# First unit's operands in tiles that are free early, more spare buffers where the left operands change, and reloaded sums in six half tiles

## The chip, the cores and the metric

The kernel runs on one core of a Trainium2 chip. A core has a matrix engine, TensorE (PE in the profile; its weight loads are PEld), and VectorE (DVE), ScalarE (ACT) and GpSimd (POOL), which work beside it in queues of their own and wait for each other by semaphores. SyncE (SP) only issues transfers, and POOL issues some too; the profile calls these two queues SPq and POOLq. Each queue runs its instructions strictly in the order in which the program wrote them. The metric is the device time of one execution in microseconds (us), lower is better. The kernel before takes 2368.73 us (median of 3 runs, 2366.69 to 2369.68).

## The reference

A gate mixes an attention branch and an MLP branch, over one sequence x of 2048 tokens and 1024 features:

```python
x = A_x                                                    # [1, 2048, 1024]
g = sigmoid((x * gate_w).sum(-1, keepdims=True))
# A: linear attention, 32 heads of 32, learned feature map
qkv = (x @ wqkv) split into q, k, v                        # wqkv [1024, 3072]
pq, pk = q @ w_phi, k @ w_phi                              # per head
phi = concat(softmax(p), softmax(-p))                      # for q and for k
kv, z = sum_s phi_k^T v, sum_s phi_k
a = (phi_q kv) / (phi_q z + 1e-6) @ wo                     # wo [1024, 1024]
# B: GEGLU
b = (gelu(x @ w_gate) * (x @ w_up)) @ w_down               # 1024 -> 3584 -> 1024
out = g * a + (1 - g) * b
```

All is float32. The kernel keeps that precision by splitting each operand into a high and a low part (`high` copies to the rounded type on ACT, `low` subtracts on DVE) and making each product in three passes: high by high, high by low, low by high.

## The kernel before, in words

**Units.** In its first part (0 to 1679 us) the kernel multiplies x by all columns of the weights for q, k, v, gate and up. After the plain products of the first 28 us (L289) the work is cut into 79 units: a unit is a pair of 128-column weight blocks by one half of the sequence. Each unit uses a Strassen-like scheme with seven products in place of eight. Its right operands, made from the weights, are x, y and z, whole tiles of 128 by 2048 values, and v, a half tile. Its left operands, made from x, are called x10, s1, s2, x11, s3, s4 and x01, a high (h) and a low (l) tile each. A product (`product`, L751) is twelve matmuls with 512 columns: four blocks of the inner dimension by three passes. The seven products go into PSUM banks named a, b, c, c11 and p, and the results of one unit seed the next: ACT copies c11 from a (L798), b from a (L800), c from b (L783), and takes p out into a tile w (L769); the second product of a unit writes the bank p again, so it waits for that copy.

**Turns.** The left operands belong to one half of the sequence and one form. Units 1 to 7 (v) are half 0, units 8 to 15 (k) half 1, units 16 to 47 half 2 (the first pass over q, gate and up), units 48 to 79 half 3 (the second pass, with the same weights). At units 8, 16 and 48, which I call turns, all seven left operands are replaced while the products go on: `PLANS` says for each one at which slot (a seventh of a unit, about 2.8 us) its float32 source is loaded, and into which home, a tile that is free just then; `change_parts` and `low_part` then split it on ACT and DVE, four pieces each.

**Sums.** In the first pass the sums x, y, z, v of each weight pair are made on DVE (L136 to L144) and stored to DRAM; the second pass loads them again. The tiles of y and z come from `slot()` (three buffers, named tyz), those of x from `new_weight()` (two buffers, named wgu). `load_part` (L596) brings y and z in two halves.

**Between the products** PE runs fillers: folds of the key and query weights with the feature matrix (L303, L443, L861), the key features times v (L971), and the attention (L1175). In the second part, from L1431 on, the output products follow, with left operands from the attention and the MLP.

**Who sets the order.** A planner in Python (`run_slot`) writes the instructions of ACT, DVE and SP beside the products. Streams (generators) offer their next step with the first slot in which it may stand, the slot in which it is due, and its estimated time on DVE and ACT; clocks of the planner decide in which slot it is written. The list `extra` places the work of the first two units by hand. An instruction written early waits at the head of its queue, and everything behind it waits too.

Of the kernel before, what the change touches and what calls it, by code (L numbers as in the profile page):

```python
# [8 lines left out]
F32 = mybir.dt.float32  # L9
# [7 lines left out]
P = 128  # L17
# [16 lines left out]
def tile_gated_mix(ctx: ExitStack, tc: tile.TileContext, x, xT, wkT, wqT, wv, w_phi, wo,  # L34
# [151 lines left out]
    with tc.manual_schedule(engines={PE, DVE, ACT, SP}):  # L186
# [140 lines left out]
        def first_sums(part):  # L327
            o, make, t = (first_o, quarter_sums, y1) if part == "y" else (first_e, more_sums, slot())
            first[part] = t
            make(first_e, first_o, True)  # L330
            high(flat(t)[0], o)
            low(flat(t)[1], o, flat(t)[0])

        def split_sums(*ks, kcs=range(1, 4)):
            for k in ks:
                for kc in kcs:
                    for do in sum_parts(k, kc):
                        do()

        def first_x():  # L340
            high(flat(x1)[0], first_e)
            low(flat(x1)[1], first_e, flat(x1)[0])

        first_x()
        for i in range(2):
            fold_piece(i)
        first_sums("y")
        for i in range(2, 4):
            fold_piece(i)
        sum_steps(100, 1)  # L350
        split_sums(0, kcs=range(4))
# [19 lines left out]
        def run_slot(t, matmuls=12, vector=0.0, scalar=0.0):  # L371
# [49 lines left out]
        def key_folds(i, groups):  # L421
            yield 14 + 4 * i, NEVER, 0.0
# [4 lines left out]
            for kc in groups:  # L427
                pieces = [(1, kc), (1, kc + 4), (0, kc), (0, kc + 4)]
                for (h, c), t in zip(pieces, four):
                    nc.sync.dma_start(t, wkT[h, c] if kc else wk_fold[h][c])  # L430
                yield now[0] + 2, NEVER, 0.0
                for n, ((h, c), t) in enumerate(zip(pieces, four)):
                    if kc == 0:
                        break
# [29 lines left out]
        def gates(pa):  # L464
# [7 lines left out]
            at = {}  # L472
# [10 lines left out]
        def change_half(t, half):  # L483
# [12 lines left out]
            for i, at, home in PLANS[half]:  # L496
                yield t + at, t + at, 0.0
                while home in busy:
                    yield now[0] + 1, now[0] + 1, 0.0
# [7 lines left out]
                busy[home] = True  # L507
# [10 lines left out]
        def home_parts(half, home):  # L518
            if half == 1:
                return (parts_of(work) if home == "y" else  # L520
                        [shared["pa"][:, n, BLK * m:BLK * m + BLK] for n in range(2) for m in range(2)])
# [265 lines left out]
        def unit(n, half, kind, m, before, extra={}):  # L787
# [5 lines left out]
            for k in range(7):  # L793
# [10 lines left out]
                for do in more_work:  # L804
                    do()
# [667 lines left out]
```

## Time and profile before

| | us |
|---|---|
| median of 3 runs (range) | 2368.73 (2366.69 to 2369.68) |
| the profiled execution | 2370.22 |
| its span, first to last instruction | 2368.4 |
| PE busy in the span | 2325.5 |
| DVE, ACT, POOL busy | 1744.5, 1210.1, 388.7 |
| mean granted TensorE clock | 0.992 |
| transfers | 645.70 MB, mean 273 GB/s |

The profiled execution's own time lies 1.5 us above the median, and its span is 1.8 us shorter than that time. PE is the engine to read: where it is idle the span grows, and where the granted clock is half, 128 by 512 matmuls start about 427 ns apart, otherwise about 227 ns. A wait is put down to the instruction that released it.

### The profile page before, as it was taken

To read this page: it belongs to the slowest core of one execution; us is meant where nothing else is said; L and a number is where in the kernel's file an instruction comes from. 1 tells how busy PE (TensorE), PEld (TensorE's weight loads), DVE (VectorE), ACT (ScalarE), POOL (GpSimd) and SP (SyncE) were. 2 spreads that over 40 slices of the span, in tenths; PEclk is the share of its full clock that TensorE was granted. 3 is DMA by queue.
4 is the path that set the end of the run, shared out by engine and by line. 5 is a ranking of instruction groups with operands and counts; after the bars stand their busy time and mean duration, and the time that the engine had idled before them with its cause. 6 is when DMAs were issued, how large, how long until landed. Compare 5 with 4: busy or idle time off the path is not lost. (4 is left out here: it accounts for less than half of the span.)

```text
span 2368.4 us, 29632 instructions
## 1 busy us (share of the span) xinstructions
PE 2325.5 (98%) x10414; PEld 1925.8 (81%) x10414; DVE 1744.5 (74%) x2394; ACT 1210.1 (51%) x1702; POOL 388.7 (16%) x618
## 2 busy tenths in 40 slices
PE   8999998999999999989999999999999999999999
PEld 6788887888888888877888888888888888888887
DVE  7667657888888887755888889875574868867873
ACT  5446346565656565543877777876433322323221
POOL 1443321222222222212111111111000000000000
PEclk9999999999999999999999999999999999999999
DMA  5689988888889999887888788877784767977874
GB/s 192 237 307 340 319 275 314 309 295 305 299 306 300 303 306 302 284 300 260 257 262 259 253 257 261 263 249 234 276 296 164 275 224 247 338 267 276 293 261 138
DMA packets 263749, 645.70 MB, mean 273 GB/s; under 512 B 32032, under 2 KB 68400, under 8 KB 255664
## 3 DMA queue, kind: packets, MB, share of 16 engines
q1 hardware_dynamic: 204592, 428.41, 54.4%
q0 software_dynamic: 58736, 215.27, 25.7%
q8 instruction: 82, 1.34, 0.2%
q14 instruction: 67, 0.55, 0.1%
q10 hardware_dynamic: 272, 0.13, 0.0%
HBM read 428.74 MB, written 215.23 MB: 272 GB/s over the span
## 5 line engine op out<-in xcount | busy, mean ns | idle before, releaser
L1431 PE MATMUL po<-tw,wgu 128*128 128x512 f32 x1344 | 309.8, 389 | 0.0
L56 ACT ACTIVATE wgu<-stage 128x1024 fp32r<-128x1024 f32 (+2 forms) x166 | 172.6, 1040 | 256.6 <-DVE stage L1321 160.9
L1431 PEld LDWEIGHTS po<-tw,wgu 128*128 128x128 f32 x1344 | 252.3, 188 | 52.4
L59 DVE TENSOR_TENSOR wgu<-stage,wgu 128x1024 fp32r<-128x1024 f32 (+2 forms) x135 | 161.5, 1196 | 87.1 <-ACT wgu L56 86.2
L751 PE MATMUL a<-s2h,tyz 128*128 128x512 f32 x632 | 212.5, 397 | 12.9 <-ACT tyz L56 5.0
L751 PE MATMUL p<-s1h,tyz 128*128 128x512 f32 x624 | 208.6, 396 | 14.0 <-DVE tyz L59 7.8
L751 PE MATMUL c<-x11h,wgu 128*128 128x512 f32 x632 | 209.7, 393 | 6.0 <-ACT x11h L56 4.3
L751 PE MATMUL c<-x01h,tyz 128*128 128x512 f32 x632 | 208.2, 390 | 0.2 <-ACT c L783 0.2
L751 PE MATMUL a<-s4h,v 128*128 128x512 f32 x632 | 208.4, 391 | 0.0
L751 PE MATMUL a<-x10h,wgu 128*128 128x512 f32 x632 | 207.9, 390 | 0.3 <-DVE wgu L59 0.3
L751 PE MATMUL b<-s3h,tyz 128*128 128x512 f32 x624 | 205.7, 390 | 0.0
L1431 PE MATMUL po<-tw,wl 128*128 128x512 f32 x672 | 156.9, 389 | 0.0
L1431 PE MATMUL po<-tyz,wgu 128*128 128x512 f32 x672 | 155.2, 389 | 0.0
L751 PEld LDWEIGHTS a<-s2h,tyz 128*128 128x128 f32 x632 | 120.4, 191 | 41.1 <-ACT tyz L56 5.4
L751 PEld LDWEIGHTS p<-s1h,tyz 128*128 128x128 f32 x624 | 118.8, 191 | 40.9 <-DVE tyz L59 9.2
L1431 PEld LDWEIGHTS po<-tw,wl 128*128 128x128 f32 x672 | 126.1, 188 | 26.2
L1431 PEld LDWEIGHTS po<-tyz,wgu 128*128 128x128 f32 x672 | 126.1, 188 | 26.2
L751 PEld LDWEIGHTS c<-x11h,wgu 128*128 128x128 f32 x632 | 119.8, 190 | 31.4 <-ACT x11h L56 4.7
L751 PEld LDWEIGHTS c<-x01h,tyz 128*128 128x128 f32 x632 | 118.8, 188 | 25.4 <-ACT c L783 0.7
L751 PEld LDWEIGHTS a<-s4h,v 128*128 128x128 f32 x632 | 119.1, 189 | 24.8
L751 PEld LDWEIGHTS a<-x10h,wgu 128*128 128x128 f32 x632 | 118.6, 188 | 25.2 <-DVE wgu L59 0.8
L751 PEld LDWEIGHTS b<-s3h,tyz 128*128 128x128 f32 x624 | 117.6, 188 | 24.1
(438 smaller groups left out, 4863.4 us busy)
## 6 DMA issues: line engine op xcount, KB each, us to landing
stage<-lm SPq DMA_DIRECT2D x98, 512.0 KB, 4.4
sr<-in_w_down SPq DMA_DIRECT2D x84, 512.0 KB, 5.0
sl<-lm SPq DMA_DIRECT2D x70, 512.0 KB, 4.7
lm<-h POOLq DMA_DIRECT2D x112, 256.0 KB, 5.7
stage<-in_w_gate SPq DMA_DIRECT2D x42, 512.0 KB, 6.7
stage<-in_w_up SPq DMA_DIRECT2D x42, 512.0 KB, 5.7
vs<-vt SPq DMA_DIRECT2D x32, 512.0 KB, 3.4
zs<-w POOLq DMA_DIRECT2D x32, 512.0 KB, 7.5
```

Source lines behind the costliest of these rows:

```text
L56: nc.scalar.activation(dst, src, AF.Copy)
L59: nc.vector.tensor_tensor(dst, src, dst_h.bitcast(F32), OP.subtract)
L751: nc.tensor.matmul(dst, w[:, h, 4 * part + kc, :], xq[e][:, kc, :], start=first and kc == 0 and i == 0, stop=kc == 3 and i == 2, skip_grou ...
L1431: nc.tensor.matmul(ps[c], lefts[s][:, a, m, c * P:(c + 1) * P], made[k][:, e, m], start=d == 0 and m == 0 and n == 0, stop=d == n_duo - 1 ...
```

## The change

**The first unit.** The x operand's high and low parts go into a tile of the pool `fa` (name s4h) in place of a weight tile, and z into a weight tile in place of a tyz tile. A fifth piece of the key weights, (1, 1), is folded early, in the tile o2. The four fold pieces no longer stand in one block behind the plain products: two pieces follow the first product, two the second, one the fourth. In the first unit the product p = s1 y stands in the third slot and not in the sixth. `extra` lists the work with costs, and the planner's clocks start at other values.

**The turns.** `PLANS` is written anew for the three turns, with other slots and homes: w is the tile `work`, y in halves 1 and 2 the shared early tile, x in half 2 three gated tiles and a tile wq. `change_parts` waits one slot more between load and split. The gates are spread over more slots; the first key features come no earlier than two slots after the turn to half 2 and not while w or y is in use. Key folds of the second kind start at slot 24 and not 18; query folds are 8/3 slots apart and not 5/3. Loads of values (`late_values`) become steps of their own.

**The second pass.** `load_part` and its callers go; a stream `reloads` loads y and z for all units from 49 on into six half tiles, each two slots after its last use. `product` then takes a half tile where there is one.

**Attention** starts later: its sums are loaded six slots after they are finished.

```diff
+        first_o = stage((0, 1024, block("v", 3)))
         room = stage().rearrange("p (a b) -> p a b", a=2)
-        first_o = stage((0, 1024, block("v", 3)))
         homes = [t[:, n] for t in (room, xa.tile([P, 2, BLK], F32, tag="v", name="fold", bufs=1)) for n in range(2)]
-        early_folds = [(h, c) for h in (1, 0) for c in (0, 4)]
+        homes.append(fa.tile([P, BLK], F32, tag="o2", name="fold", bufs=1))
+        early_folds = [(h, c) for h in (1, 0) for c in (0, 4)] + [(1, 1)]
...
-        x1 = new_weight()
         y1 = xa.tile([P, 2, KC, P], F32R, tag="pts", name="first", bufs=1)
         for i in (1, 2, 4, 5):
-            x_ops[0, i] = [x_part(i, part) for part in range(2)]
+            x_ops[0, i] = [x_part(i, part) if i != 5 else None for part in range(2)]
+        x1 = fa.tile([P, 2, KC, P], F32R, name="s4h", bufs=1)
...
+        def first_high(part, src):
+            if part == "z":
+                first[part] = new_weight()
+            high(flat(first[part])[0], src)
+
+        def first_low(part, src):
+            low(flat(first[part])[1], src, flat(first[part])[0])
+
+        def sums_high(k, *kcs):
+            if x_ops[0, (1, 2, 4, 5)[k]][0] is None:
+                x_ops[0, 5] = [x_part(5, part) for part in range(2)]
+            for kc in kcs:
+                sum_parts(k, kc)[0]()
+
+        def sums_low(k, *kcs):
+            for kc in kcs:
+                sum_parts(k, kc)[1]()
+
+        first_high("x", first_e)
+        first_low("x", first_e)
+        sums_high(0, 0, 1, 2)
+        quarter_sums(first_e, first_o, True)
+        first_high("y", first_o)
+        sums_low(0, 0, 1, 2)
         sum_steps(100, 1)
-        split_sums(0, kcs=range(4))
+        sums_high(0, 3)
+        first_low("y", first_o)
+        sums_low(0, 3)
...
-                    d *= 0.95
+                    d *= 0.97
...
-            yield 14 + 4 * i, NEVER, 0.0
+            yield 14 + 10 * i, NEVER, 0.0
...
-                yield max(now[0], at[c] + 3), NEVER, 1.3
+                yield max(now[0], at[c] + 3, begin + 9 * c // 8), NEVER, 1.3
...
-                while home in busy:
+                while home in busy or half == 2 and (gating[0] if home in ("w", "y") else folding[0]):
...
-        held_homes = []
-        SPARE = ((0, -7, "x"), (1, -6, "y"), (2, -4, "x"), (3, -3, 2), (4, -1, "y"))
-        PLANS = {1: (*SPARE, (6, 0, "x"), (5, 3, "y")), 3: (*SPARE, (6, 0, "g"), (5, 3, "z")),
-                 2: ((0, -11, "x"), (2, -5, 1), (1, -5, "x"), (3, -1, "x"), (4, 0, 3), (5, 3, 6), (6, 4, "x"))}
+        held_homes, gating = [], [True]
+        PLANS = {1: ((0, -9, "x"), (1, -8, "w"), (2, -5, "x"), (3, -4, "w"), (4, -1, "x"), (6, 1, "w"), (5, 3, "x")),
+                 2: ((0, -9, "w"), (1, -8, "y"), (2, -5, "w"), (3, -5, "x"), (4, -4, "y"), (6, 0, "w"), (5, 3, "x")),
+                 3: ((0, -7, "x"), (1, -5, "y"), (2, -4, "x"), (3, -3, "z"), (4, -1, 3), (5, 0, "g"), (6, 3, "z"))}
...
+                if j == 3 and raw[3] is raw[0]:
+                    yield now[0] + 3, need - 2, 0.0
...
-                else:
-                    yield max(now[0], t - 4), t - 4, 0.0
-                    y = mine["y"] = slot()
-                    load_part("y", y, 0)
-                    yield max(now[0], t - 2), t - 2, 0.0
-                    load_part("y", y, 1)
...
-            else:
-                yield t, t, 0.0
-                z = mine["z"] = slot()
-                load_part("z", z, 0)
-                yield t + 1, t + 1, 0.0
-                load_part("z", z, 1)
...
+        def reloads(n):
+
+            uses = sorted((7 * m + at, m, i, part) for m in range(n, len(units))
+                          for at, i, part in ((1, "y", 0), (3, "z", 0), (6, "y", 1), (9, "z", 1)))
+            rooms, t = [], 7 * n
+            last = len(uses) - 1
+            for k, (at, m, i, part) in enumerate(uses):
+                before = k - 6 if k < last - 1 else k - 4
+                if k < 6:
+                    if k % 2 == 0:
+                        yield t + (-4, 1, 4)[k // 2], NEVER, 0.0
+                        while k == 0 and "y" in busy:
+                            yield now[0] + 1, NEVER, 0.0
+                        whole = slot()
+                        rooms += [whole[:, :, 4 * h:4 * h + 4] for h in range(2)]
+                    room = rooms[k]
+                else:
+                    yield uses[before][0] + 2, NEVER, 0.0
+                    room = rooms[k % 6] = rooms[before % 6]
+                nc.sync.dma_start(room.rearrange("p a b c -> p a (b c)").bitcast(F32),
+                                  sums[units[m][1:]][i].rearrange("p (a b) -> p a b", a=2)[:, :, BLK * part:BLK * part + BLK])
+                right_ops[m][i, part] = room
...
+                elif k == 2:
+                    product(n, p, "y", 0, 1, half, True)
                 elif k == 3:
                     product(n, a, "z", 0, 2, half)
                 elif k == 4 and before:
                     product(n - 1, unit_banks[n - 1][0], "v", 0, 5, before[0])
-                elif k == 5:
-                    product(n, *((c11, "x", 1, 3, half) if before else (p, "y", 0, 1, half, True)))
+                elif k == 5 and before:
+                    product(n, c11, "x", 1, 3, half)
...
-                yield max(now[0], 62 + 5 * n // 3), NEVER, 0.0
+                yield max(now[0], 60 + 8 * n // 3), NEVER, 0.0
...
-                if fjobs and now[0] >= fjobs[0][0] and not folding[0]:
+                if fjobs and now[0] >= max(fjobs[0][0], 7 * TURNS[1] + 2) and not folding[0] and not {"w", "y"} & set(busy):
...
+            def late_values(after):
+                loaded[0] = False
+                yield now[0] + 1, now[0] + 1, 0.0
+                load_values(*after)
+                loaded[0] = True
...
+            sums_at[0] = now[0] + 6
...
-        tensor[0] = 35.0
-        clock[:] = 47.0, 42.0
-
-        outs, puts = ([lambda n=n, at=at, do=do: do(n, *at) for n, at in enumerate(((1, 0), (0, 1), (0, 0), (1, 1)))]
-                      for do in (plain_out, plain_store))
+        start(reloads(TURNS[-1] + 1))
+        tensor[0] = 22.0
+        clock[:] = 25.0, 23.6
+
+        outs, puts = ([(lambda n=n, at=at, do=do: do(n, *at), *cost) for n, at in enumerate(((1, 0), (0, 1), (0, 0), (1, 1)))]
+                      for do, *cost in ((plain_out, 0.0, 0.6), (plain_store, 0.84, 0.8)))
+        folds = [(lambda i=i: fold_piece(i), 0.0, 0.6, 0.95) for i in range(len(homes))]
         extra = {
             1: {0: [outs[0]],
-                1: [outs[1], lambda: sum_steps(100, 3), lambda: split_sums(1, 2, 3, kcs=(0,)), lambda: first_sums("z"), lambda: split_sums(1)],
-                2: [outs[2], outs[3]],
-                4: [lambda: split_sums(2)],
-                5: [lambda: sum_steps(1), lambda: split_sums(3, kcs=(1,))]},
-            2: {0: puts[:2], 1: [lambda: sum_steps(100), lambda: split_sums(3, kcs=(2, 3))], 2: puts[2:]}}
+                1: [*folds[:2], (lambda: more_sums(first_e, first_o, True), 1.4), (lambda: first_high("z", first_e), 0.0, 1.05),
+                    (lambda: sum_steps(2, 3), 1.4), (lambda: first_low("z", first_e), 1.2), (lambda: sum_steps(100, 3), 2.8),
+                    outs[1], (lambda: sums_high(1, *range(4)), 0.0, 2.4), (lambda: sums_low(1, *range(4)), 2.6)],
+                2: [*folds[2:4], (lambda: sums_high(2, *range(4)), 0.0, 2.4), (lambda: sum_steps(1), 0.7),
+                    (lambda: sums_high(3, 0), 0.0, 0.6), (lambda: sums_low(2, *range(4)), 2.6), (lambda: sums_low(3, 0), 0.7)],
+                4: [*folds[4:], outs[2], outs[3]]},
+            2: {1: [(lambda: sum_steps(1), 0.7), (lambda: sums_high(3, 1), 0.0, 0.6), (lambda: sums_low(3, 1), 0.7)],
+                2: [(lambda: sum_steps(100), 1.4), (lambda: sums_high(3, 2, 3), 0.0, 1.2), (lambda: sums_low(3, 2, 3), 1.4)],
+                3: puts[:1], 5: puts[1:2]},
+            3: {1: puts[2:3], 2: puts[3:]}}
```

What follows are rows of the three queues at the places of which the prediction speaks, in the order in which each queue runs them. The first is ACT's queue behind the plain products, before; `tyz<-stage` is the high part of z, `first<-stage` that of y, `s1h` to `s4h` are left operands, and `stage<-misc`, `fold<-misc` take the folds out.

```order
L56 ACTIVATE wgu<-stage 128x1024
L56 ACTIVATE stage<-misc 128x512 x2
L56 ACTIVATE first<-stage 128x1024
L56 ACTIVATE fold<-misc 128x512 x2
L56 ACTIVATE s1h<-raw 128x512 x4
L56 ACTIVATE w_545<-c_85 128x512
L798 ACTIVATE c_85<-a 128x512
L56 ACTIVATE w_545<-b 128x512
L56 ACTIVATE s2h<-raw 128x512
L56 ACTIVATE s3h<-raw 128x512
L56 ACTIVATE s4h<-raw 128x512
L56 ACTIVATE tyz<-stage 128x1024
```

And now:

```order
L56 ACTIVATE s4h<-stage 128x1024
L56 ACTIVATE s1h<-raw 128x512 x3
L56 ACTIVATE first<-stage 128x1024
L56 ACTIVATE s1h<-raw 128x512
L56 ACTIVATE w_547<-c_85 128x512
L815 ACTIVATE c_85<-a 128x512
L56 ACTIVATE stage<-misc 128x512 x2
L56 ACTIVATE wgu<-stage 128x1024
L56 ACTIVATE w_547<-b 128x512
L56 ACTIVATE s2h<-raw 128x512 x3
```

The folds' copies moved behind the copy of c11, and z's high part (now in wgu) stands ahead of the pieces of s2, s3 and s4.

The second place is ACT's queue at the turn to half 3, before; `x01h<-w` are the pieces of the left operand x01, `w_544<-p` frees the bank p.

```order
L56 ACTIVATE x01h<-w_544 128x512
L800 ACTIVATE b<-a 128x512
L56 ACTIVATE x01h<-w_544 128x512 x3
L56 ACTIVATE s4h<-stage 128x512 x4
L723 ACTIVATE h<-c_85 128x512
L769 ACTIVATE w_544<-p 128x512
```

And now:

```order
L817 ACTIVATE b<-a 128x512
L56 ACTIVATE wgu<-stage 128x1024
L56 ACTIVATE s4h<-w_546 128x512 x3
L56 ACTIVATE x01h<-stage 128x512 x4
L738 ACTIVATE h<-c_85 128x512
L786 ACTIVATE w_546<-p 128x512
L800 ACTIVATE c<-b 128x512
L815 ACTIVATE c_85<-a 128x512
L56 ACTIVATE s4h<-w_546 128x512
```

x01 has a home of four pieces, and the operand with a home of three is s4, whose fourth piece moved behind the copy of p and two more copies.

The third place is SP's queue early in the second pass, before; tq1y and tq1z are the stored sums y and z of the second q pair, `wgu<-tq2x` is x of the third, zs is the attention's sums.

```order
L64 DMA stage<-wq_187 128x1024
L612 DMA wgu<-tq2x 128x1024
L596 DMA tyz<-tq1z 128x2x512
L1031 DMA zs<-zs_172 128x1024
L1031 DMA zs<-zs_173 128x1024
L596 DMA tyz<-tq1z 128x2x512
L682 DMA o_8479<-wq_186 128x512
L596 DMA tyz<-tq2y 128x2x512
```

And now:

```order
L702 DMA tyz<-tq0z 128x2x512
L702 DMA tyz<-tq1z 128x2x512
L702 DMA tyz<-tq1y 128x2x512
L678 DMA v<-tq0v 128x512
L702 DMA tyz<-tq2y 128x2x512
L64 DMA stage<-wq_187 128x1024
L616 DMA wgu<-tq2x 128x1024
```

The first half of tq1z moved ahead of the loads of the third pair's weights, of v of the first and of the attention's sums.

More of the change, by code (lines that the diff above doesn't have):

```diff
@@ L560, in low_part @@
             low(dst, x, h)
-            if j == KC // 2 - 1:
+            busy[home] -= 1
+            if not busy[home]:
                 del busy[home]
@@ L750, in product @@
                 for i, (h, e) in enumerate(PASSES):
-                    nc.tensor.matmul(dst, w[:, h, 4 * part + kc, :], xq[e][:, kc, :], start=first and kc == 0 and i == 0,
+                    nc.tensor.matmul(dst, w[:, h, kc, :], xq[e][:, kc, :], start=first and kc == 0 and i == 0,
                                      stop=kc == 3 and i == 2, skip_group_check=True)
@@ L975, in accumulate @@
                     if after:
[L976 removed]
+                        start(late_values(after))
                     if j:
@@ L981, in push @@
                     yield now[0], NEVER, 0.0
-                    while j == 0 and not bank_free[0]:
+                    while j == 0 and not bank_free[0] or not loaded[0]:
                         yield now[0] + 1, NEVER, 0.0
```

72 lines of the change are left out of this document (27 added, 45 removed).

## The prediction

> **What bounds the kernel now.** I read the share of PE first, then PE's waits, then the busy time by stage. From the page's first part (the span is 2368.4 us):
>
> ```profile
> PE 2325.5 (98%) x10414; PEld 1925.8 (81%) x10414; DVE 1744.5 (74%) x2394; ACT 1210.1 (51%) x1702; POOL 388.7 (16%) x618
> ```
>
> PE is the bound: idle for 2368.4 - 2325.5 = 42.9 us of the span. The change adds no matmul, so all it can win is that idle time and what half clock costs behind it. PE's waits (engine, line, what it waited for: total, times, longest):
>
> ```profile
> PE p L751 <- DVE tyz L59: 7.8, 3, 5.1
> PE p L751 <- ACT w L769: 6.2, 2, 5.3
> PE a L751 <- ACT tyz L56: 5.0, 1, 5.0
> PE c L751 <- ACT x11h L56: 4.3, 1, 4.3
> PE a L751 <- DMA tyz<-tq1z: 3.0, 1, 3.0
> PE misc L971 <- issue: 2.8, 1, 2.8
> PE a L751 <- DMA tyz<-tq2z: 2.6, 1, 2.6
> PE a L751 <- DVE tyz L59: 0.8, 1, 0.8
> PE a L751 <- DMA tyz<-tg3z: 0.5, 1, 0.5
> ```
>
> Nearly all is in three places. Busy time by stage (stretch, its length, PE busy with its matmuls, PEld, DVE, ACT, POOL, granted clock, DMA share, GB/s):
>
> ```profile
> 28.00:72.00 44.00, 30.89 (x125) 23.52 (x124) 33.39 (x54) 25.26 (x47) 10.29 (x16) 0.84 0.50 160
> 340.00:392.00 52.00, 43.91 (x178) 34.25 (x177) 35.34 (x51) 33.15 (x56) 9.60 (x15) 0.93 0.88 314
> 392.00:940.00 548.00, 548.00 (x2518) 457.68 (x2518) 449.86 (x586) 322.25 (x424) 131.55 (x218) 1.00 0.88 303
> 940.00:1000.00 60.00, 59.16 (x273) 49.09 (x272) 46.74 (x65) 28.93 (x43) 17.22 (x26) 1.00 0.88 280
> 1000.00:1106.00 106.00, 92.41 (x383) 75.16 (x382) 51.72 (x77) 39.15 (x69) 16.86 (x28) 0.92 0.81 283
> 1679.00:2368.00 689.00, 685.47 (x3025) 567.25 (x3023) 480.53 (x482) 208.92 (x217) 16.18 (x30) 1.00 0.73 255
> ```
>
> The first pass (392 to 940) has no idle time at all, and the output part next to none: 689 / 3025 = 0.228 us a matmul, so 2.73 for a product of twelve. The idle time is 44 - 30.89 = 13.1 in the first unit, 52 - 43.91 = 8.1 at the turn to half 2, 106 - 92.41 = 13.6 at the turn to half 3.
>
> Behind the long waits the clock is half. The same view, cut just behind each:
>
> ```profile
> 42.20:49.00 6.80, 5.27 (x12) 3.67 (x13) 3.32 (x5) 4.53 (x7) 0.00 (x0) 0.50 0.67 194
> 62.60:69.40 6.80, 4.46 (x11) 3.49 (x12) 6.18 (x12) 5.10 (x11) 2.90 (x4) 0.50 0.79 263
> 364.80:371.60 6.80, 6.80 (x32) 5.61 (x31) 1.88 (x3) 0.63 (x1) 1.08 (x2) 1.00 0.94 355
> 376.70:383.50 6.80, 5.07 (x11) 3.71 (x12) 4.99 (x7) 5.60 (x9) 1.04 (x2) 0.50 0.87 318
> 1008.10:1011.50 3.40, 2.77 (x11) 2.61 (x12) 2.26 (x3) 1.06 (x3) 0.54 (x1) 0.50 1.00 386
> 1038.80:1045.60 6.80, 4.62 (x11) 3.65 (x12) 4.08 (x6) 4.04 (x8) 1.08 (x2) 0.50 0.69 274
> 1073.00:1076.40 3.40, 3.40 (x10) 2.65 (x9) 3.32 (x5) 0.00 (x0) 0.00 (x0) 0.50 0.99 359
> 1096.90:1100.30 3.40, 3.40 (x10) 2.63 (x9) 1.92 (x4) 0.70 (x2) 0.54 (x1) 0.50 0.83 320
> ```
>
> How far apart the matmuls then start, from the order of time of PE (start, duration, instruction, their number):
>
> ```profile
> 1041.57 0.63 PE L751 MATMUL p<-s1l,tyz 128*128 128x512 f32 x1
> ...
> 1044.56 1.05 PE L751 MATMUL p<-s1h,tyz 128*128 128x512 f32 x2
> ```
>
> Seven starts in 2.99 us are 0.427 each, 0.2 more than at full clock. I charge these 0.2 us to every matmul in the rows at 0.50: first unit 23 x 0.2 = 4.6, turn to half 2 11 x 0.2 = 2.2, turn to half 3 42 x 0.2 = 8.4. In all the three places lose 17.7, 10.3 and 22.0, with 0.8 near 960 and 0.5 for tg3z 51.3 us; 2370.2, the profiled execution's own time, less 51.3 is 2319.
>
> The row at 364.80 stands behind a wait of p of 1.8 us and has full clock; the shortest wait with half clock behind it is the 2.6 of tq2z. So a left-over wait under 2 us costs itself, one over 2.6 about 1.6 to 2.4 more. The Trainium skill (TensorE: Matmul & The Clock Gate, Part 1) puts the fall after at least one idle window of about 3.4 us, the window running free. By that rule the waits of 2.6, 2.8 and 3.0 would have left the clock alone, and the sum would be 31 x 0.2 = 6.2 us smaller; the rows show half clock behind all three, in stretches of 3.4, so I go by the rows.
>
> **The first unit.** DVE's and ACT's order of time while PE waits, and the price of the values' splits and of the folds in this stage:
>
> ```profile
> 35.66 1.28 DVE L149 TENSOR_TENSOR raw<-raw 128x512 f32<-128x512 f32 x2
> ...
> 41.80 0.69 DVE L144 TENSOR_TENSOR stage<-stage 128x512 f32<-128x512 f32 x1
> ```
>
> ```profile
> 42.58 1.06 ACT L56 ACTIVATE tyz<-stage 128x1024 fp32r<-128x1024 f32 x1 [4.89 <-DVE stage L144]
> ```
>
> ```profile
> L167 DVE TENSOR_TENSOR w<-w,w 128x256 fp32r<-128x256 f32 x6 | 2.4, 421 | 1.1 <-ACT w L164 1.1
> L303 PE MATMUL misc<-bp,fold 128*128 128x128 f32 x16 | 2.0, 279 | 0.0
> ```
>
> z's sums (L141, L144) stood behind nine operations of 0.64 us each (two in 1.28); hence the 5.0 of a. In the changed order z's sums and high part stand ahead of the pieces of s2, s3 and s4, which removes about 41.8 - 35.7 = 6 us of that path, more than the wait. The 5.1 of p in unit 2 was y's low part behind the splits of the values (L167, 0.42 each, with waits for ACT's halves), which are now written half a unit to a unit later. One fold piece more, four matmuls or 2.0 / 4 = 0.5 us of PE, is done here and saved at unit 8: nothing in sum. Laying the new order out with these durations I find three waits: 1.0 at b (ACT's copy b stands behind a large high part), 1.8 at p for the low part of y, 2.2 at a of unit 2 for z's low part, whose queue now holds what was moved. That is 5.0 of 17.7 left, all under 2.6: a gain of 12.7. Bounds: if the three go, 17.7; if each grows beyond 2.6 and halves the clock (3 x 2.0 more), 6.7. I take 13.
>
> **The turn to half 2.** ACT's order of time:
>
> ```profile
> 377.02 0.63 ACT L56 ACTIVATE s3h<-x11l 128x512 fp32r<-128x512 f32 x1 [1.98 <-DMA x11l<-xs]
> 377.55 2.18 ACT L56 ACTIVATE x11h<-w 128x512 fp32r<-128x512 f32 x4
> ```
>
> x11h, for which PE waited 4.3, stood behind s3h's pieces, which waited for loads. Homes w and y let s1 and x10 load and split before the turn, s3 goes into a home of its own (x) at -5, and the first features leave the stretch, whose DVE was busy for 35.33 of 52. In my layout each piece of s3 and x11 is ready 6 us or more before its product. The work is not gone: features that leave here are paid by DVE in 392 to 940, busy 449.86 of 548, with 98 us to spare. Gain 10 of 10.3; at worst one wait of 4.3 with half clock stays (6.5), so 4.
>
> **The turn to half 3 and the reloads.** ACT and SP in order of time, and the loads with their landing times (calls, KB, median us to landing) between 1010 and 1040:
>
> ```profile
> 1037.26 0.63 ACT L56 ACTIVATE x01h<-w 128x512 fp32r<-128x512 f32 x1 [7.91 <-DMA w<-in_xT]
> ```
>
> ```profile
> 1027.28 0.34 SPq L553 DMA_DIRECT2D w<-in_xT  x1
> ...
> 1068.98 0.53 SPq L596 DMA_DIRECT2D tyz<-tq1z  x1
> ```
>
> ```profile
> tyz<-tq0y SPq DMA_DIRECT2D x2, 512.0 KB, 10.7
> ```
>
> The fourth piece of x01 was issued at 1027.28 and landed ten us later, and ACT's copy of p behind it came late: 5.3. Now the late fourth piece is s4's, behind the copies of p, c and c11, so PE no longer waits for it in that place; x01 has a full home. tq1z was issued at 1068.98 and waited for at 1071.9. A half tile is now issued two slots after the use of six halves earlier; four halves in a unit of seven slots make that 10.5 - 2 = 8.5 slots, 8.5 x 2.73 = 23 us ahead, against a landing of up to 10.7. Waits for tq1z, tq2z and tg3z go: 6.1 with 20 x 0.2 = 4. In my layout 1 us stays at p for tq0y in the crowded queue and 1.2 at the features. Gain 22.0 + 0.5 - 2.2 = 20; I take 18, since two waits here have margins under 3 us. At worst the loads stay crowded: see the second rival.
>
> **The rest.** The wait near 960 goes (0.8). The tail of the attention moves. PE's order of time:
>
> ```profile
> 1639.88 0.84 PE L1175 MATMUL misc<-pts,kbs 128*128 128x512 f32 x3
> ...
> 1678.87 1.07 PE L1431 MATMUL po<-tyz,wgu 128*128 128x512 f32 x4
> ```
>
> The last attention ended 39 us before the output products; now fewer than three products, about 8 us, lie between. Copies, divisions and stores that those 39 us covered run beside the first output products, whose operand is late by 0 to 2 us in my layout. I charge 1, and keep 6 (one 3.4 wait at half clock) as the bound. Sum: 13 + 10 + 18 + 0.8 - 1 = 40.8, and 2370.2 - 40.8 = 2329.4. The median lies 1.5 below the profiled time; against that I leave 1 us for short waits that a layout by mean durations does not see. I forecast **2329**.
>
> **The rivals.**
> 1. *All that is lost comes back:* 2319 less the 1.5 to the median, 2317. For it: 548 us without idle time in the first pass, with DVE at 82%. Against: every stretch with new operands shows a wait.
> 2. *The turn to half 3 stays bound by the transfers.* Its 106 us moved 283 GB/s x 106 = 30.0 MB; without the 22 us lost they would have to fit in 84, 357 GB/s. The stretches 1008 and 1073 show 386 and 359, so the queues are near full there. If the loads that moved only raise that stretch to the 303 GB/s of the first pass, 30.0 MB take 99 us: 15 of the 22 stay lost, and not 4, and the time is 2329 + 11 = 2340. Against: seven left operands start earlier, into 940 to 1000 with 280 GB/s. The Trainium skill (DMA: Bandwidth & Descriptors, Specifications) gives a limit of about 358 GB/s from HBM per core. By it the 84 us would just hold the bytes; the trace shows 386 over 3.4 us, so it doesn't bind there as a hard ceiling.
> 3. *The tail comes late:* the output products wait 5 to 8 us, with half clock 2 more: 2337. The 39 us of before hid this chain; I know its parts only by mean durations.
> 4. *Slower:* SP's queue is one file. A half-tile load waits there until PE has left the half; were it written too early, each load behind it would come late. Price: a wait of 2.6 and 8 x 0.2 of half clock, 4.2, in each of 31 units is 130, less the 23 won elsewhere: 2369 + 107 = 2476, and over the old time from six such units on. It decides when SP is held more than 23 - 10.7 = 12 us. For it: in the old trace SP does wait long for PE:
>
> ```profile
> SPq L686 <- PE a L751: 17.3, 2, 8.9
> ```
>
> 8.9 is the longest, under 12.
>
> **How the numbers follow.** Forecast 0.54, rival 1 0.12, rival 2 0.16, rival 3 0.08, rival 4 0.06, and 0.04 that stalls merely move and the time stays. Runs spread over 3 us, so 0.2%, 4.7 us, is about what can be told from no change. The forecast's own range is 2321 to 2337: 8 us to either side is about what one of the three gains can miss by (13 against 6.7 to 17.7, 10 against 4). For 8 in 10 I reach over rivals 1, 2 and 3: 2314 to 2348, a little beyond them on both sides for the bounds of the first unit. Faster 0.90, same 0.04, slower 0.06.
>
> **What would show it right or wrong.** Right: PE busy for over 38 of the 44 us from 28 to 72; no stretch at half clock in 340 to 392; no wait for tq1z, tq2z or tg3z; between 1000 and 1106 at most one wait over 2.6; PE busy in all near 2325.5 - 15.2, the half clock gone. Wrong: waits over 2.6 with half clock behind them in the first 60 us (step one), for x11h or s3h (step two), for left operands behind SP (rival 2), or before L1468 (rival 3).

## The result and the profile after

The changed kernel takes 2342.82 us (median of 4 runs, 2338.67 to 2344.95) against 2368.57 us before (4 runs, 2366.69 to 2369.68): ratio 0.989, 95% interval 0.9873 to 0.9907. It is faster by 25.8 us; 39.7 were forecast (2329). The time lies in the range of 2314 to 2348, but outside the 2321 to 2337 that the prediction called the forecast's own, and it is nearest to the second rival's 2340. The profiled execution took 2341.32 us with a span of 2339.5.

The page's first part, after:

```profile
PE 2314.3 (99%) x10414; PEld 1916.1 (82%) x10414; DVE 1745.1 (75%) x2394; ACT 1212.6 (52%) x1703; POOL 388.7 (17%) x618
```

PE's idle time fell from 42.9 to 2339.5 - 2314.3 = 25.2 us, its busy time by 2325.5 - 2314.3 = 11.2 with the same number of matmuls and a mean granted clock of 1.000 in place of 0.992: that is the half clock that went. 17.7 + 11.2 = 28.9 is the whole difference of the two spans. PE's waits after (line L768 is the product, L1205 the attention, L1468 the output products):

```profile
PE misc L1205 <- DVE pts L59: 3.8, 5, 0.8
PE p L768 <- DVE tyz L59: 3.2, 3, 1.3
PE c L768 <- ACT c L800: 2.7, 1, 2.7
PE a L768 <- DVE h L781: 2.6, 1, 2.6
PE a L768 <- DVE tyz L59: 2.5, 2, 1.9
PE p L768 <- ACT w L786: 1.6, 3, 0.9
...
PE misc L1205 <- ACT pts L56: 1.0, 2, 0.7
PE po L1468 <- DVE wgu L59: 0.7, 1, 0.7
```

None of the long waits of before is left, and no wait is over 2.7; in their place stand twenty or so short ones, several of which the kernel before did not have. By stage, with the columns as before:

```profile
28.00:72.00 44.00, 42.14 (x211) 34.90 (x210) 35.92 (x60) 28.33 (x54) 12.76 (x20) 1.00 0.60 203
72.00:340.00 268.00, 264.00 (x1261) 221.23 (x1261) 171.15 (x277) 128.59 (x225) 102.54 (x151) 1.00 0.91 309
340.00:392.00 52.00, 50.79 (x223) 41.30 (x222) 36.71 (x52) 32.64 (x52) 11.21 (x19) 1.00 0.96 358
1000.00:1106.00 106.00, 99.34 (x440) 80.93 (x440) 57.50 (x91) 46.65 (x72) 19.19 (x32) 1.00 0.87 303
1300.00:1660.00 360.00, 354.63 (x1547) 289.16 (x1546) 285.81 (x473) 255.96 (x372) 48.62 (x77) 1.00 0.77 242
1660.00:2339.00 679.00, 674.44 (x2973) 557.47 (x2972) 476.29 (x477) 207.85 (x216) 15.10 (x28) 1.00 0.73 256
```

Two stretches of before that the prediction did not show, since they had next to no idle time:

```profile
72.00:340.00 268.00, 267.76 (x1293) 225.30 (x1292) 167.41 (x274) 123.57 (x219) 102.80 (x151) 1.00 0.86 298
1300.00:1660.00 360.00, 359.07 (x1583) 296.59 (x1582) 287.09 (x484) 261.46 (x385) 49.67 (x78) 1.00 0.81 253
```

Idle time before and after: first unit 13.1 and 1.9; 72 to 340 us 0.2 and 4.0; turn to half 2 8.1 and 1.2; turn to half 3 13.6 and 6.7; 1300 to 1660 us 0.9 and 5.4. The three places gave what they had, nearly; two quiet stretches began to lose.

What happened at 1033, where c waits 2.7, is seen in four queues in order of time. SP waits 10.0 us for PE to free the values' tile (vs) and then issues that load and seven more within 6 us:

```profile
1016.23 0.33 SPq L940 DMA_DIRECT2D vs<-vt  x1
...
1022.18 1.00 SPq L616 DMA_DIRECT2D wgu<-tq2x  x1
```

```profile
SPq L940 <- PE misc L1001: 10.0, 1, 10.0
```

Loads and stores issued between 1016 and 1024, us to landing in the last column:

```profile
wgu<-tq2x SPq DMA_DIRECT2D x1, 512.0 KB, 12.8
q<-h POOLq DMA_DIRECT2D x2, 256.0 KB, 10.6
```

The store of q holds its result tile h, DVE waits for that tile, ACT for DVE, PE for ACT:

```profile
1032.14 0.69 DVE L781 TENSOR_TENSOR h<-b,w 128x512 f32<-128x512 f32 x1 [4.50 <-DMA q<-h]
1032.87 0.58 ACT L800 ACTIVATE c<-b 128x512 f32<-128x512 f32 x1 [7.10 <-DVE h L781]
```

The wait of 2.6 for h at 1088 is another thing. There h waits for no store: DVE waits 9.95 for a load of q, works off the attention's steps from 1078.58 to 1087.7 without a gap, and only then, in the order of its queue, takes the bank a out into h:

```profile
1078.58 0.71 DVE L1106 STREAM_TRANSPOSE stage<-qx 128x512 f32<-128x512 f32 x1 [9.95 <-DMA qx<-q]
...
1087.71 0.69 DVE L781 TENSOR_TENSOR h<-a,w 128x512 f32<-128x512 f32 x1
```

### The profile page after: what moved, and what is told of

Its sections match the earlier page's. It is cut to its first block, busy times and chain, and to the rows that moved or that the text cites. A ratio compares the mean times of both kernels' runs of the same rounds, so it can differ in the third digit from the quotient of the medians.

```text
span 2339.5 us, 29686 instructions
## 1 busy us (share of the span) xinstructions
PE 2314.3 (99%) x10414; PEld 1916.1 (82%) x10414; DVE 1745.1 (75%) x2394; ACT 1212.6 (52%) x1703; POOL 388.7 (17%) x618
## 5 line engine op out<-in xcount | busy, mean ns | idle before, releaser
L1468 PE MATMUL po<-tw,wgu 128*128 128x512 f32 x1344 | 309.8, 389 | 0.0
L1468 PEld LDWEIGHTS po<-tw,wgu 128*128 128x128 f32 x1344 | 252.3, 188 | 52.4
L768 PE MATMUL p<-s1h,tyz 128*128 128x512 f32 x624 | 205.7, 391 | 4.9 <-DVE tyz L59 3.2
L768 PE MATMUL a<-s2h,tyz 128*128 128x512 f32 x624 | 205.6, 390 | 3.5 <-DVE tyz L59 2.5
L768 PE MATMUL c<-x01h,tyz 128*128 128x512 f32 x624 | 206.1, 391 | 2.8 <-ACT c L800 2.7
L768 PE MATMUL a<-x10h,wgu 128*128 128x512 f32 x624 | 205.6, 390 | 2.6 <-DVE h L781 2.6
L768 PE MATMUL a<-s4h,v 128*128 128x512 f32 x632 | 207.7, 389 | 0.0
L768 PE MATMUL b<-s3h,tyz 128*128 128x512 f32 x624 | 205.5, 390 | 0.0
L768 PE MATMUL c<-x11h,wgu 128*128 128x512 f32 x624 | 205.0, 389 | 0.0
L1468 PE MATMUL po<-tyz,wgu 128*128 128x512 f32 x672 | 155.7, 389 | 1.2 <-DVE wgu L59 0.7
L1468 PE MATMUL po<-tw,wl 128*128 128x512 f32 x672 | 156.9, 389 | 0.0
L1468 PEld LDWEIGHTS po<-tyz,wgu 128*128 128x128 f32 x672 | 126.0, 188 | 28.2 <-DVE wgu L59 1.2
L1468 PEld LDWEIGHTS po<-tw,wl 128*128 128x128 f32 x672 | 126.1, 188 | 26.2
L768 PEld LDWEIGHTS p<-s1h,tyz 128*128 128x128 f32 x624 | 116.8, 188 | 31.8 <-DVE tyz L59 4.9
L768 PEld LDWEIGHTS a<-s2h,tyz 128*128 128x128 f32 x624 | 117.0, 188 | 29.1 <-DVE tyz L59 3.3
L768 PEld LDWEIGHTS c<-x01h,tyz 128*128 128x128 f32 x624 | 117.2, 188 | 28.0 <-ACT c L800 4.2
L768 PEld LDWEIGHTS a<-x10h,wgu 128*128 128x128 f32 x624 | 117.2, 188 | 27.6 <-DVE h L781 3.5
L768 PEld LDWEIGHTS a<-s4h,v 128*128 128x128 f32 x632 | 118.6, 188 | 24.5
L768 PEld LDWEIGHTS b<-s3h,tyz 128*128 128x128 f32 x624 | 117.2, 188 | 24.3 <-ACT b L817 0.4
L768 PEld LDWEIGHTS c<-x11h,wgu 128*128 128x128 f32 x624 | 117.1, 188 | 24.3
```

The source lines that it names most:

```text
L768: nc.tensor.matmul(dst, w[:, h, kc, :], xq[e][:, kc, :], start=first and kc == 0 and i == 0, stop=kc == 3 and i == 2, skip_group_check=True)
L1468: nc.tensor.matmul(ps[c], lefts[s][:, a, m, c * P:(c + 1) * P], made[k][:, e, m], start=d == 0 and m == 0 and n == 0, stop=d == n_duo - 1 ...
```

## The experiments

There are two theories. A: the parts of the change add up, each has removed its own waits. B: after the long waits a stage is limited by something shared (transfers, result tiles, VectorE), so what one part wins another gives back. Groups ran with their own runs of the kernel before (medians 2368.7, 2370.3, 2367.6, 2369.9), so across groups I compare ratios; 0.001 is 2.4 us. With intervals of about 0.0013 to either side, two ratios are told apart from about 0.002 on, which is 5 us.

**The changed kernel again.**

> The changed kernel unchanged, as the yardstick of this group. Both theories: 2338 to 2345 us, as in its four runs so far; 0.9873 to 0.9907 of the kernel before.

2345.53 us, ratio 0.9898 (0.9883 to 0.9913). This is the yardstick.

**First unit as before.** The edit puts back the old tiles, the block of folds and the old start of the clocks:

```diff
+        x1 = new_weight()
...
-        x1 = fa.tile([P, 2, KC, P], F32R, name="s4h", bufs=1)
...
-        tensor[0] = 22.0
-        clock[:] = 25.0, 23.6
+        tensor[0] = 35.0
+        clock[:] = 47.0, 42.0
```

> The changed kernel with the first unit as before (x in a weight tile, folds in one block, planner clocks 35, 47, 42). Theory A, the parts add up: the stage from 28 to 72 us loses its 13 us of idle time and 2 to 4 of half clock again, and the new waits of 2.7 us that the trace shows for unit 3 (72 to 90 us) go: 2343 + 13 = 2356. Theory B, part of the first unit's gain was already given back by what follows, up to unit 8: 2343 + 6 = 2349.

2357.91 us, 12.4 more than the yardstick. The stage is back to its old picture, with an idle time of 44 - 30.70 = 13.3 and a clock of 0.88:

```profile
28.00:72.00 44.00, 30.70 (x132) 23.64 (x130) 33.55 (x54) 25.77 (x48) 10.35 (x16) 0.88 0.50 162
```

Theory A: this part is worth 12 to 13 us by itself.

**Reloads as before**, and, in another kernel, **the plan of the turn to half 3 as before**:

```diff
+                    y = mine["y"] = slot()
+                    load_part("y", y, 0)
...
-        start(reloads(TURNS[-1] + 1))
```

```diff
-                 3: ((0, -7, "x"), (1, -5, "y"), (2, -4, "x"), (3, -3, "z"), (4, -1, 3), (5, 0, "g"), (6, 3, "z"))}
+                 3: ((0, -7, "x"), (1, -6, "y"), (2, -4, "x"), (3, -3, 2), (4, -1, "y"), (6, 0, "g"), (5, 3, "z"))}
```

> The changed kernel with y and z loaded as before, in whole tiles two or three slots ahead. Theory A, each wait of before for tq1z, tq2z and tg3z (3.0, 2.6, 0.5) comes back with half clock behind the first two, about 9 us, and nothing else moves: 2352. Theory B, the early reloads are also what delays the stores of q near 1020 us (seven loads issued in 6 us, c waits 2.7): that wait goes, so only about 5 us are lost: 2348.

> The changed kernel with the plan of loads at the turn to half 3 as before (x01 in the home of three pieces, s1 in a tyz tile at -6, x11 in s2l, s4 in a tyz tile at -1). Theory A, the order of homes is what removed the wait of p (5.3 and 2.2 of half clock): it comes back, 2350. Theory B, the transfers set the time there: the wait of p comes back smaller or larger with the queue, 3 to 10 us beside it at the reloads, which need the tyz tile that s1 and s4 now hold: 2355 or more.

2343.97 and 2344.31 us, 0.9891 (0.9878 to 0.9905) and 0.9893 (0.9879 to 0.9906): neither costs anything that the runs can tell, and a cost of over about 3 us lies outside the intervals. PE's waits with the old reloads:

```profile
PE a L784 <- DMA tyz<-tq0z: 4.2, 1, 4.2
PE a L784 <- DMA tyz<-tq2z: 2.1, 1, 2.1
```

The waits for sums do come back, but the waits of c and of a for h (3.2 and 3.0 in the yardstick's profile) shrink to 0.4 together, and those of the attention from 5.2 to 2.3. With the old plan of the turn PE waits 2.2 for tq0y, 0.4 for c and not for h, and the attention's waits grow to 8.5. Both expectations of theory A fell, and so did the rival's times, 2348 and 2355; of theory B the first run bears out only that the waits of c and h shrink.

**Both as before.**

> The changed kernel with both the plan of the turn to half 3 and the loads of y and z as before; each alone cost nothing (2344.3 and 2344.0 against 2345.5). Theory A, the two stand in for each other: with both undone the turn loses its 13 us of idle time and half clock again, 2357. Theory B, neither is what freed the turn; it is the rest of the change, which moved features and gates: 2343 to 2348.

2345.12 us, 0.9897 (0.9884 to 0.9909): still nothing that the runs can tell, as theory B had it. So the two don't stand in for each other. PE's waits:

```profile
PE p L784 <- DMA tyz<-tq0y: 2.9, 1, 2.9
PE a L784 <- DMA tyz<-tq1z: 2.0, 1, 2.0
```

The 5.3 of p behind the fourth piece of x01 is not among them, though x01 has its home of three pieces again.

**Both as before, and without the pause.** Besides one slot more between load and split, what was left of the change in the split of x01 are two lines in `change_parts`:

```diff
-                if j == 3 and raw[3] is raw[0]:
-                    yield now[0] + 3, need - 2, 0.0
```

> The kernel with both the plan of the turn to half 3 and the reloads as before, and now also without the pause of three slots ahead of the fourth piece of an operand whose home has three (two lines of the change). ScalarE's queue again has all four pieces of x01 ahead of the copy of p. Theory A, that pause is what freed the turn: the wait of p for the fourth piece comes back, 5 us and 2 of half clock, 2345 + 7 = 2352. Theory B, the gates and features that moved away freed transfers and VectorE there: the fourth piece lands early enough, at most 2 us are lost, 2347.

The wait of before is back, to the tenth of a us, with half clock behind it (0.50 over the next 3.4 us). ACT's late fourth piece of x01 again stands ahead of the copy of p:

```profile
PE p L782 <- ACT w L800: 6.1, 4, 5.3
```

```profile
1012.37 0.63 ACT L56 ACTIVATE x01h<-w 128x512 fp32r<-128x512 f32 x1 [7.61 <-DMA w<-in_xT]
...
1013.38 0.59 ACT L800 ACTIVATE w<-p 128x512 f32<-128x512 f32 x1
```

So with the old plan the pause of three slots, which puts the fourth piece behind the copy of p, is what removes it. Whether the new plan needs the pause too was not run. The time is 2345.83 us, 0.9899 (0.988 to 0.9917): not slower than with the pause. Between the two profiles 4.4 us of idle time came up in 1000 to 1106, with the half clock, and 3.4 went between 1106 and 1660, where the attention's waits for DVE fell from 3.3 to 1.8; the medians don't tell the two kernels apart. Theory A is right on the mechanism, theory B on the time.

**Turn to half 2 and features as before** (plan, homes, pace of gates and folds, start of the features):

```diff
-                if fjobs and now[0] >= max(fjobs[0][0], 7 * TURNS[1] + 2) and not folding[0] and not {"w", "y"} & set(busy):
+                if fjobs and now[0] >= fjobs[0][0] and not folding[0]:
```

> The changed kernel with the plan of the turn to half 2, the pace of gates and query folds and the start of the features as before. Theory A, the parts add up: the turn to half 2 loses its 8 to 9 us again and nothing else moves, 2354. Theory B, the later features also cost the attention its head start (its last product group is again 14 products ahead of the output products and not 3), so the waits of L1205 between 1300 and 1660 us (5 us) go: 2349. Theory B of the run before says also that the turn to half 3 gets worse by up to 13: 2362.

2354.74 us, 0.9937 (0.9924 to 0.9949), 0.0039 or 9 us more than the yardstick: theory A's 2354. The wait of before is back:

```profile
PE c L768 <- ACT x11h L56: 4.4, 1, 4.4
PE misc L1205 <- DVE pts L59: 5.8, 8, 0.8
```

The second row falls against theory B: the attention has its head start again (its last group stands 38 us ahead of the output products), and its groups wait as before or more. The expectation's 2362, for a turn to half 3 that gets worse without the moved features and gates, fell too: that turn's idle time is 106 - 100.81 = 5.2, against 8.1 in the yardstick.

**Filler time mended.** The waits of L1205 have a cause in the planner. A group is written where its time plus a margin lies ahead of the product's end; as its time, `push` took that of its own empty step, the begin of the slot, and not the end of the low part on DVE. In the trace of the changed kernel DVE starts that low part at 1325.51, PE reaches the group at 1325.53:

```profile
1325.51 1.22 DVE L59 TENSOR_TENSOR pts<-w,pts 128x1024 fp32r<-128x1024 f32 x1 [3.65 <-ACT pts L56]
```

```profile
1325.53 0.51 PE L1205 MATMUL misc<-pts,kbs 128*128 128x512 f32 x1
1326.78 0.50 PE L1205 MATMUL misc<-pts,kbs 128*128 128x512 f32 x1 [0.75 <-DVE pts L59]
```

```diff
-                if k != 0 and fillers and fillers[0][0] + OVER < tensor[0] + 12 * PART and k in fillers[0][3]:
+                if k != 0 and fillers and fillers[0][0] + 2.7 < tensor[0] + 12 * PART and k in fillers[0][3]:
...
-                    start(push())
+                    start(push(), passed[0])
```

> The changed kernel, in which the planner writes an attention or feature product group only where the low part of its operand is ready by its own clock before the product it follows has ended (it took the begin of the slot for that time). Theory A, the waits of L1205 (5 to 8 waits of 0.3 to 1.8) come from groups written one product too early: they go, 5 to 6 us, 2340. Theory B, VectorE is late there because result tiles h wait for their stores, and the groups wait wherever they stand: 2345.

2337.81 us, 0.9866 (0.9853 to 0.9878): faster than the yardstick by 0.0032, 7.6 us (0.0024, 5.7 us, against the changed kernel's first four runs), and the best of all. No wait of L1205 is left. The stretch in question, first in the yardstick, then here:

```profile
1300.00:1640.00 340.00, 334.26 (x1456) 273.50 (x1455) 277.42 (x466) 247.61 (x360) 45.39 (x71) 0.99 0.78 244
```

```profile
1300.00:1640.00 340.00, 338.93 (x1486) 277.94 (x1485) 279.20 (x465) 266.55 (x378) 45.58 (x72) 1.00 0.79 248
```

5.7 us of idle time became 1.1. Theory A. The edit mends the time and also raises the margin (`OVER`) from 1.0 to 2.7; no run has one without the other, so it stays open which of them moves the groups far enough.

**Values later.** Each load of values, the one for which SP was held 10.0 us among them, is written two slots later:

```diff
-                yield now[0] + 1, now[0] + 1, 0.0
+                yield now[0] + 3, now[0] + 3, 0.0
                 load_values(*after)
```

> The changed kernel with the load of the values two slots later behind the product group that frees their tile. In the trace SyncE waits 10.0 us there near 1010 us and then issues seven loads in 6 us. Theory A, this hold bunches the loads and so delays the store of q, the tile h and c (2.7 near 1033): the wait of c goes, 2342. Theory B, the queue is full there anyway and the wait moves: 2345.

2346.17 us, 0.99 (0.9885 to 0.9914): no gain. The wait of c shrinks to 0.7, as theory A says, and the wait for h goes, since here h stands among the attention's steps on DVE (at 1084.27) and not behind them. The turn's idle time shrinks from 6.7 in the first profile of the changed kernel, and 8.1 in the yardstick's, to 106 - 104.57 = 1.4:

```profile
1000.00:1106.00 106.00, 104.57 (x468) 86.29 (x467) 55.45 (x85) 47.48 (x73) 18.91 (x31) 1.00 0.93 320
```

```profile
PE misc L1205 <- DVE pts L59: 5.0, 7, 0.9
PE misc L1001 <- DMA vs<-vt: 2.1, 1, 2.1
```

But features wait for the values, and the attention's waits, in an order that the planner wrote anew, are 7.4 (with 2.4 for ACT) against the yardstick's 5.2. What was won at the turn does not reach the end: theory B on the time, though the order and not the transfers takes back what can be seen. By stage the account closes: against the yardstick 6.7 us of idle time went at the turn, while 2.1 came up in 940 to 1000 (the wait for the values), 3.4 in 1106 to 1300 (2.3 of it waits of the attention), and 1.5 in the other stages, 7.0 in all.

**Three edits together.** Filler time mended, the old plan of turn 3, and in unit 3 later stores of the plain products' values; a and b differ in these:

```diff
-            3: {1: puts[2:3], 2: puts[3:]}}
+            3: {1: puts[2:3], 4: puts[3:]}}
```

> The changed kernel with the filler time mended, the plan of the turn to half 3 as before, and the last store of the plain products' values three slots later in unit 3. Theory A, the waits are independent: 2337.8 less 3 (h at 1034 and 1090 against tq0y) and 2 (z's low part in unit 3), 2333. Theory B, the reloads' first half, held up by s1 and s4 in a tyz tile, and the stores that now fall on unit 4 take back the same: 2337.

> The same with the last two stores of the plain products' values in the fourth and fifth slot behind unit 3's start, both behind z's low part. Theory A: the wait for z's low part in unit 3 (2.4) goes whole, 2332. Theory B: the splits now stand ahead of unit 4's y and x, which come late by as much: 2335 or more.

a: 2342.19 us, 0.9883 (0.9862 to 0.9904); b, with `{4: puts[2:3], 5: puts[3:]}`: 2347.94, 0.9907. Both are slower than theory A's 2333 and 2332, and a is slower than theory B's 2337 too. They fail at the same place, in a:

```profile
PE misc L1205 <- DVE pts L59: 5.2, 1, 5.2
PE a L768 <- DVE tyz L59: 1.0, 1, 1.0
```

The wait for z's low part did shrink, from 2.4 in the mended kernel to 1.0. But with these edits the planner put the last attention group directly ahead of the output products, where there is no product left to hide it: 5.2 and half clock behind it. The third version moves the planner's factor on DVE's durations from 0.97 to 0.96, which puts that group seven products earlier.

```diff
-                    d *= 0.97
+                    d *= 0.96
```

> The same edits as three_mended_a, with the planner's factor on VectorE's durations at 0.96 in place of 0.97, which brings the last attention group from directly ahead of the output products to seven products ahead of them. Theory A, the 5.2 us wait of that last group with half clock behind it (about 7 us in all) was the only loss of that kernel against its lead of 6 us at the end of the units: 2342 - 7 = 2335 or a little less. Theory B, every factor writes another order with its own waits, so the loss comes back elsewhere: 2338 to 2345.

2345.79 us, 0.9893 (0.9876 to 0.9909): theory B, just above its 2338 to 2345. The wait at the end went, and the new order has waits of its own:

```profile
PE p L768 <- ACT w L786: 6.3, 9, 1.6
PE a L768 <- ACT c L815: 3.5, 4, 1.4
PE misc L1205 <- DVE pts L59: 1.3, 2, 0.8
```

## Why the prediction was right or wrong

The direction, the range and the list of the three places were right; the gain was 28.9 in the profiles where 40.8 were summed. The range held because it reached over the second rival, and that rival's 2340 is near by luck: it priced 15 us lost at the turn to half 3, where 6.7 stayed, and the rest of the shortfall came up elsewhere. Term by term:

- **First unit: right in size, wrong in place.** 5.0 of idle time were to stay; 1.9 stayed between 28 and 72, but 2.7 came up right behind it: the splits of the values, moved from unit 2 to unit 3, stand there ahead of z's low part (a waits 1.9), and p waits 0.8. I had laid that wait out for unit 2. Another 1.3 for y's low part, near 199 us, is 1.1 in the kernel with the old first unit, so it comes from some other part of the change, behind the turn to half 1, which I had not looked at. Undoing the part costs 12.4 against 13 forecast.
- **Turn to half 2: right.** 10 forecast; its idle time fell by 6.9 with the half clock behind it, and undoing it, with the features, costs 9, which the runs do not tell from 10.
- **Turn to half 3: the reason was partly wrong.** I credited the home of x01 and the early reloads. Undone, alone and together, they cost nothing that the runs can tell. With the old plan the pause ahead of the fourth piece, which I had read only as a detail of s4, is enough to keep the 5.3 of p away; so x01's full home was not needed for it. The reloads do remove the waits for sums, as laid out, but not for 18 us: with SP held by the load of the values, they are issued in a burst, the store of q lands after 10.6, and c waits 2.7 behind a tile h. That is the second rival's crowding, with the mechanism of the fourth (one file on SP) under its 12 us. The other 2.6, at 1088, are the order of DVE's queue. 6.7 of idle time stayed where I had left 4. What else freed that turn (with both undone the profile still shows 106 - 100.13 = 5.9 idle against 13.6 before) was not taken apart. The features and gates that moved are not it by themselves: with them as before, and the new plan and reloads, 5.2 stay. All of these undone at once was not run.
- **The rest: the step that failed most.** The shortfall that weighs most is a term that the sum put at nothing. I checked the last attention group alone (1 us charged; its stretch lost 1.0 more, 4.6 against 3.5) and took the 31 others as unchanged. They moved by several products, and 1300 to 1660 lost 4.4 us more. The cause lies in where the planner places a group, by a time that is too early and with a margin of 1.0; changing both gives 6 to 8 us.
- **Half clock: mis-sized.** 76 matmuls at 0.2 us made 15.2; 11.2 were there to win, 0.15 each. The rows themselves say so: their busy time less 0.227 us for each of the 76 is 11.7. Their counts take in matmuls that a row's edge cuts, and eight of the eleven in the row at 1008.10 are L971's, with 256 columns and not 512.

In sum, 4.0 of half clock, 3.8 of idle time between 72 and 340 us, 4.4 in the attention, 2.7 at turn 3 and 0.9 at turn 2, less the 3.1 that the first unit did better, are 12.7 and cover the missing 11.9; most of the difference is 0.9 that went unforecast in 1106 to 1300.

The fourth rival was set aside on a reading that is wrong for the trace as a whole. I gave 8.9 as SP's longest wait for PE; that holds for the second pass, where the reloads stand, but the same view has longer ones, for the values' tile, all before 943 us:

```profile
SPq L918 <- PE misc L971: 409.5, 31, 14.1
```

So the margin under 12 us was thinner than I wrote. In the changed kernel's second pass the longest wait of SP for PE is the 10.0 at 1006, and the rival did not come about.

## What to carry to other kernels

When a planner writes the order, an edit moves groups far from its place: compare the waits of the quiet stretches too, since work that had a product or two of room there may lose it. What a part wins at its own place can be lost again in the order that the planner then writes for the rest, as with the values and the pause, so undo each part before crediting it, and close the account stage by stage. And what removes a long wait may be the smallest line of the diff.

## What the runs showed of the hardware

The forecast held that waits under 2 us leave the clock alone and waits over 2.6 halve it. The runs show no such line. Rows of 3.40 us just behind a wait; in the changed kernel, behind waits of 2.69 and 2.58:

```profile
1033.50:1036.90 3.40, 3.40 (x15) 2.80 (x16) 0.47 (x1) 1.72 (x3) 0.25 (x1) 1.00 1.03 365
1088.50:1091.90 3.40, 3.40 (x15) 2.83 (x16) 2.28 (x2) 1.58 (x2) 0.54 (x1) 1.00 1.02 397
```

In the kernel with the filler time mended, behind the same two waits, now 2.75 and 2.94:

```profile
1033.10:1036.50 3.40, 3.37 (x10) 2.70 (x11) 0.33 (x1) 1.43 (x2) 0.29 (x1) 0.68 1.02 359
1089.70:1093.10 3.40, 3.39 (x8) 2.75 (x9) 2.33 (x2) 1.58 (x2) 0.54 (x1) 0.50 1.04 402
```

And in the changed kernel's second profile, behind a wait of only 1.99:

```profile
82.10:85.50 3.40, 3.40 (x10) 2.66 (x11) 3.12 (x5) 1.07 (x2) 2.01 (x3) 0.62 0.89 292
```

Behind waits of about 1.5 to 3.0 the clock sometimes fell and sometimes not (it fell behind 1.51 in the kernel with the values later, and held behind 2.99 in the yardstick); behind the eleven of 4.2 and more in the fourteen traces it fell each time. Fifteen matmuls start in 3.40 us at full clock and eight at half, so one such fall costs about 7 x 0.227 = 1.6 us.

What looks like chance is mostly the place of the wait on a grid. In each trace all changes of the granted clock lie a whole number of 3.413 us apart, and where that grid lies differs from one execution to the next. Cut into the cells of its grid, a wait of 2.7 may fall into two cells or into one. In the changed kernel the 2.69 is split, and PE is busy for half of the cell; in the kernel with the filler time mended the 2.75 lies nearly whole in one cell, and the next cell is at half clock:

```profile
1029.13:1032.55 3.42, 1.68 (x8) 1.06 (x6) 0.41 (x1) 0.00 (x0) 0.86 (x1) 1.00 1.03 398
```

```profile
1030.93:1034.34 3.41, 1.20 (x5) 1.03 (x6) 0.69 (x1) 1.84 (x3) 0.62 (x1) 1.00 1.10 379
1034.34:1037.76 3.42, 3.42 (x9) 2.67 (x9) 1.33 (x2) 0.30 (x2) 0.00 (x0) 0.50 0.68 259
```

Taken over all fourteen traces (the first 30 and the last 15 us left out), half clock followed on all 28 cells at full clock in which PE was busy for under 0.43 of the cell, on 9 of the 28 between 0.43 and 0.55, and on none of the 9322 above. The Trainium skill (TensorE: Matmul & The Clock Gate, Part 1) has the window run free, which agrees with the grid, and puts the fall after at least one idle window of about 3.4 us; in these traces a cell in which PE was busy for a third of the time was enough. Such falls may be a part of why the changed kernel's runs spread over 6 us with waits of 2 to 3 us in them; that was not tested.
